# Multiplying the first 256 tokens of a softplus layer in whole fp32, and splitting its operands for later blocks only

## The chip, the cores and the metric

One core of one Trainium2 chip runs the whole program. The metric is the device time in microseconds (us), the median of several executions. Lower is better. "The profile" is the record of one execution by the hardware profiler.

## What is computed

Three layers, all on 1536 tokens (2 sequences of 768). First a gated linear recurrence per head (8 heads of 48) with a complex decay; its output is the x of the next layer. Then a feed-forward layer with softplus between its two products, and last four experts with relu, weighted per token:

```python
for t in range(S):
    S_re, S_im = ar * S_re - ai * S_im + kv, ar * S_im + ai * S_re
    y[:, :, t] = np.einsum('bhd,bhde->bhe', q[:, :, t], S_re)
...
h = x @ w_in
g = np.maximum(h, 0.0) + np.log1p(np.exp(-np.abs(h)))
x = g @ w_out
...
for e in range(4):
    out += p[:, e:e + 1] * (np.maximum(x @ w1[e], 0.0) @ w2[e])
```

Everything is fp32. d_model is 384, the softplus layer is 2048 wide, each expert 1024.

## The kernel before, in words

**Stages.** The work of the two feed-forward layers is cut into twelve stages k (k 0 to 5 for the first sequence, 6 to 11 for the second; s = k % 6). s 0 and 1 are the two halves of the softplus layer's 2048 columns, s 2 to 5 the experts. A stage has eight slices f of 128 columns and two blocks of 384 tokens; stage 0 alone has three blocks of 256 tokens, since the recurrence is still delivering its chunks of 128 tokens while it runs. Block 0 is the first 256 tokens.

**Split products.** TensorE multiplies in fp32r. To keep fp32's accuracy, each operand is a sum of a high and a low half, and a product is three matmuls (high x high, low x high, high x low). `part` (L179) makes the halves of a weight: ScalarE casts it to the high half (L181), VectorE subtracts that from the weight (L182). `done` (L718) does the same for x, out of PSUM (L721, L722), and `second` (L265) for the softplus values g (L275, L276). The recurrence itself (transposes L674, scores L683, mixes L699, states L710, prefix sums L593) multiplies in whole fp32.

**A stage's steps.** `step` (L366) runs `first` (the first product, L232, into the PSUM tile h, which holds a pair of slices f in stage 0; then |h|, exp and log on ScalarE and the maximum and sum on VectorE, L250), `second` for the step before (the split of g), and `third` for the step three before (the second product, L314, into the tile y). `low_sum` (L258) adds up one slice of g as a check.

**Weights.** The softplus weights come from memory as 64-bit numbers. `conv` (L195) joins the two words of each into an fp32 number with three VectorE operations (`join`, L69, into a scratch tile f of two buffers), splits it, and writes the joined number to a scratch tensor in memory (L200), from where stages 6 and 7 read it again. A weight of 768 columns (n even: first product, "A"; n odd: second product, "B") is converted in two halves of 384. High and low lie together in one of nine slots (NR) of a ring; three of stage 1's weights lie in a separate pool.

**Order.** The program is one list of units, sorted by a position written out by hand (`events`, `put`, `run`, L758 to L767), and each engine works through its instructions in that order. Position p is the p-th step of stage 0 for p from 0 to 24 (8 to a block); stage 1 begins at 24, stage 2 at 40. The weights of stage 0 are loaded at -5.2 + 1.6n and converted 0.4 and 0.8 later, those of stage 1 from 8.3 + 2.3n, each not before its slot is free by `ring` (L845 to L854). The recurrence's chunks are put between by position too (L863 to L868); each chunk's x comes out of `done`. All loads here are issued by SP, in the same order.

Of the kernel before, what the change touches and what calls it, by code (L numbers as in the profile page):

```python
# [9 lines left out]
F32 = mybir.dt.float32  # L10
F32R = mybir.dt.float32r
# [9 lines left out]
LAG = 3  # L21
# [15 lines left out]
NR = 9  # L37
# [38 lines left out]
def fast_path(ctx: ExitStack, tc, bad, wsc, qkv, a_re, a_im, w_in, w_out, probs, w1, w2, out):  # L76
# [83 lines left out]
    def weights(k, n, tile):  # L160
        s, which, j = k % 6, n % 2, n // 2
        nm = f"{'AB'[which]}{k}_{j}"
        z = {}

        def slot():
            t = tile([P, 2, KT, 256] if which == 0 else [P, 2, 2, DM], F32R, nm)
            W[k, n] = t
            z["d"] = t.rearrange("p s a b -> p s (a b)")

        def load():  # L170
            slot()
            if s >= 2:
                src = (w1, w2)[which][s - 2, j]
            else:
                src = wsc[s * 8 + n]
            z["raw"] = tmp.tile([P, 768], F32, tag="raw", name="raw" + nm, bufs=4)
            nc.sync.dma_start(z["raw"], src)

        def part(src, sl):  # L179
            hi, lo = (z["d"][:, i, sl] for i in range(2))  # L180
            nc.scalar.copy(hi, src)  # L181
            nc.vector.tensor_tensor(lo, src, hi.bitcast(F32), ALU.subtract)  # L182

        if k >= 2:
            return [load, lambda: part(z["raw"], slice(0, 768))]

        def load2():
            slot()
            z["raw"] = []
            for h in range(2):  # L190
                raw = tmp.tile([P, HW, 2], I32, tag="raw", name=f"raw{nm}_{h}", bufs=4)
                nc.sync.dma_start(raw.rearrange("p a w -> p (a w)"), w_raw[which][s * 4 + j, h])
                z["raw"].append(raw)

        def conv(h):  # L195
# [22 lines left out]
    def gemm1(k, blk, f):  # L218
# [10 lines left out]
        n = 0  # L229
        for kk in range(KT):  # L230
            for (p, q) in ((0, 0), (1, 0), (0, 1)):
                nc.tensor.matmul(ps, wt[:, p, kk, o:o + P], XB[b][:, q, kk, tok], start=(n == 0), stop=(n == 3 * KT - 1))  # L232
                n += 1
        return ps

    def first(k, blk, f):
# [4 lines left out]
        if k % 6 < 2:  # L241
# [7 lines left out]
            act(t, t, AF.Ln, bias=b_one)  # L249
            nc.vector.scalar_tensor_tensor(t, h, 0.0, t, ALU.max, ALU.add)  # L250
# [14 lines left out]
    def second(k, blk, f):  # L265
# [3 lines left out]
        if k == 0:  # L269
            if f % 2 == 0:  # L270
                return
# [19 lines left out]
    def third(k, blk, f):  # L291
# [15 lines left out]
        for j in range(nj):  # L307
            for n, (p, q) in enumerate(((0, 0), (0, 1), (1, 0))):
                if s < 2:
                    l_, r_ = wt[:, q, f % 2, j * P:(j + 1) * P], g[p] if k == 0 else g[:, p, :]  # L310
                else:
                    l_, r_ = g[:, p, j * P:(j + 1) * P], wt[:, q, f % 2, :]
                mate = k == 0 and j == 1
                mm = nc.tensor.matmul(ys[j], l_, r_, start=(opens and n == 0 and not mate),  # L314
                                      stop=(closes and n == 2), skip_group_check=k == 0)
# [33 lines left out]
    def closing(j):  # L349
# [4 lines left out]
        for i, sl in enumerate(parts):  # L354
            ps = psum.tile([P, 512], F32, tag="a" if i == 0 else "h", name=f"ya{j}_{i}", bufs=3 - i)[:, :sl.stop - sl.start]
            for f in range(HALF, FH):
                wt = W[k, f // 2 * 2 + 1]
                for n, (p, q) in enumerate(((0, 0), (0, 1), (1, 0))):
                    nc.tensor.matmul(ps, g_t[k, blk, f][:, p, j * P:(j + 1) * P], wt[:, q, f % 2, sl],  # L359
# [57 lines left out]
    def part(k, j, q):  # L417
# [3 lines left out]
        def prod(ps, w, x, start=False, stop=False):  # L421
            lt, li = (raws, w) if w < 5 else (sums, w - 5)
            for n, (p, r) in enumerate(((0, 0), (1, 0), (0, 1))):
                rhs = XC[b][:, r, x, :] if isinstance(x, int) else halves(b, *x, r)
                nc.tensor.matmul(ps, lt[:, p, li, :], rhs, start=(start and n == 0), stop=(stop and n == 2),  # L425
# [48 lines left out]
    def fast_weights(k, n):  # L474
# [4 lines left out]
        def load():  # L479
            z["raw"] = tmp.tile([P, 768], F32, tag="raw", name="raw" + nm, bufs=4)  # L480
            nc.sync.dma_start(z["raw"], (w1, w2)[which][s - 2, j])
            t = slot([P, 2, KT, 256] if which == 0 else [P, 2, 2, DM], F32R, nm)
            if which == 1:
                W[k, n] = t
                z["d"] = t.rearrange("p s a b -> p s (a b)")
            else:
                z["d"] = t.rearrange("p s a b -> p (s a b)")[:, :10 * P].rearrange("p (s i c) -> p s i c", s=2, i=5)
# [5 lines left out]
        def second_layer():  # L493
            split(z["d"][:, 0], z["d"][:, 1], z["raw"])

        def plain():
            r, d = z["raw"].rearrange("p (a b) -> p a b", a=KT), z["d"]
            split(d[:, 0, 0:3], d[:, 1, 0:3], r[:, :, :P])
            split(d[:, 0, 3:5], d[:, 1, 3:5], r[:, 0:3:2, P:])

        def sums():
# [9 lines left out]
            W[k, n] = (z["d"], t)  # L511
# [143 lines left out]
    def s3_units(n, c):  # L655
# [62 lines left out]
        def done():  # L718
            hi, lo = (XB[b][:, i, :, cc * P:(cc + 1) * P] for i in range(2))
            ysr = z["y"][:, :3 * P].rearrange("p (j t) -> p j t", t=P)  # L720
            nc.scalar.copy(hi, ysr)  # L721
# [46 lines left out]

    s1_load(0)
# [34 lines left out]
    def slot(shape, dt, nm):  # L804
        return wp.tile(shape, dt, tag="w", name=nm, bufs=NR)

    def spare(shape, dt, nm):
        return early.tile(shape, dt, tag=nm, name=nm)
# [4 lines left out]
    for m, k in enumerate(ORDER):  # L813
# [27 lines left out]
        for n in range(8):  # L841
            if k == 0:
                pos, gap = -5.2 + 1.6 * n, 0.4
            elif k == 1:
                pos, gap = 8.3 + 2.3 * n, 0.6  # L845
            else:
                pos, gap = base[m - 1] + 1 + 1.7 * n, 1.5
            in_early = k == 1 and n in (2, 3, 4)
            if not in_early:
                if len(ring) >= NR:  # L850
                    pos = max(pos, ring[len(ring) - NR] + 0.1)
                ring.append(base[m + 1] - FH + 2 * (n // 2) + 1 + (LAG if n % 2 else 0))
            for i, u in enumerate(weights(k, n, spare if in_early else slot)):
                events.append((pos + gap * i, len(events), u))  # L854
    for pos, need, last, k, n in sorted(fast_events):
        pos = max(pos, ring[len(ring) - NR] + 0.1)
        ring.append(last)
# [305 lines left out]
```

## Time and profile before

| | us |
|---|---|
| median of 3 executions | 736.29 (735.73 to 737.26) |
| span of the profiled execution, first to last instruction | 736.2 |
| TensorE busy | 703.0 (95%) |
| VectorE busy | 584.7 (79%) |
| ScalarE busy | 487.0 (66%) |

The profile lists no other time of its execution than the span. PE is TensorE, PEld its weight loads, DVE VectorE, ACT ScalarE, POOL GpSimd, SP the queue that issues most transfers. TensorE's records overlap one another, and their ends are modelled, so a busy share near 100% is not TensorE at its peak; the time from one record's start to the next one's is the better price. A whole-fp32 matmul (other than a transpose) has two records, an fp32r matmul one.

### The profile page before, as it was taken

To read this page: it belongs to the slowest core of one execution; us is meant where nothing else is said; L and a number is where in the kernel's file an instruction comes from. 1 tells how busy PE (TensorE), PEld (TensorE's weight loads), DVE (VectorE), ACT (ScalarE), POOL (GpSimd) and SP (SyncE) were. 2 spreads that over 40 slices of the span, in tenths; PEclk is the share of its full clock that TensorE was granted. 3 is DMA by queue.
4 is the path that set the end of the run, shared out by engine and by line. 5 is a ranking of instruction groups with operands and counts; after the bars stand their busy time and mean duration, and the time that the engine had idled before them with its cause. 6 is when DMAs were issued, how large, how long until landed. Compare 5 with 4: busy or idle time off the path is not lost.

```text
span 736.2 us, 13313 instructions
## 1 busy us (share of the span) xinstructions
PE 703.0 (95%) x5171; PEld 676.2 (92%) x5171; DVE 584.7 (79%) x1150; ACT 487.0 (66%) x898; POOL 33.3 (5%) x31
## 2 busy tenths in 40 slices
PE   1688999999999999999999999999999999999996
PEld 0477899999899999999999999999999999999996
DVE  6999999955875854648888779988788899988963
ACT  7887886878896856345686666555556667666640
POOL 1132010000111011000000000000000000000000
PEclk9699999999999999999999999999999999999998
DMA  7655666721211420121022130213454445554501
GB/s 264 195 175 170 230 190 195 228 84 44 75 55 59 122 81 2 59 86 44 23 86 65 29 102 21 87 44 98 128 159 146 137 151 172 151 172 140 172 32 69
DMA packets 36486, 83.56 MB, mean 113 GB/s; under 512 B 4544, under 2 KB 13376, under 8 KB 36416
## 3 DMA queue, kind: packets, MB, share of 16 engines
q1 hardware_dynamic: 36128, 82.35, 35.5%
q8 instruction: 42, 0.69, 0.4%
q10 hardware_dynamic: 288, 0.30, 0.1%
q14 instruction: 28, 0.23, 0.1%
HBM read 73.95 MB, written 8.65 MB: 112 GB/s over the span
## 4 chain that ended last, share of the span: by engine, by line
PE 70%; DVE 10%; DMA 9%; ACT 8%; issue 2%; POOL 1%; SPq 0%; ACTq 0%; POOLq 0%; DVEq 0%
PE y L314 21%; PE h L232 18%; PE z L314 9%; PE px L425 7%; PE pv L425 3%; PE tp L674 2%; DMA rawB<-in_w_dram 2%; DMA chkw<-in_w_in_dram 2%; PE pc L425 2%; PE sp L683 2%; PE yps L699 2%; DMA chki<-in_a_im_dram 1%; PE ya L359 1%; PE sps L710 1%; DVE fA L72 1%
## 5 line engine op out<-in xcount | busy, mean ns | idle before, releaser
L232 PE MATMUL h<-X,A 128*128 128x384 f32 (+1 forms) x936 | 176.1, 329 | 2.5 <-ACT A L181 0.8
L232 PEld LDWEIGHTS h<-X,A 128*128 128x128 f32 x936 | 153.4, 188 | 5.8 <-issue 1.6
L314 PE MATMUL y<-B,g 128*128 128x384 f32 x744 | 150.0, 335 | 0.0
L314 PEld LDWEIGHTS y<-B,g 128*128 128x128 f32 x744 | 131.1, 188 | 0.5 <-issue 0.2
L314 PE MATMUL y<-g,B 128*128 128x384 f32 (+1 forms) x504 | 91.0, 315 | 0.3 <-ACT g L285 0.3
L314 PE MATMUL z<-B,g 128*128 128x384 f32 x372 | 84.7, 334 | 0.0
L314 PEld LDWEIGHTS y<-g,B 128*128 128x128 f32 x504 | 79.3, 189 | 1.9 <-ACT g L285 0.6
L314 PEld LDWEIGHTS z<-B,g 128*128 128x128 f32 x372 | 66.3, 188 | 0.0
L247 ACT ACTIVATE e<-h 128x384 f32<-128x384 f32 (+1 forms) x60 | 30.8, 513 | 37.3 <-PE h L232 36.3
L250 DVE SCALAR_TENSOR_TENSOR e<-h,e 128x384 f32<-128x384 f32 (+1 forms) x60 | 34.9, 581 | 21.0 <-ACT e L103 20.1
L255 DVE SCALAR_TENSOR_TENSOR g<-h,g 128x384 fp32r<-128x384 f32 x32 | 17.7, 554 | 28.2 <-ACT g L254 28.2
L103 ACT ACTIVATE e<-e,b_one 128x384 f32<-128x384 f32 (+1 forms) x60 | 38.2, 637 | 1.3
L103 ACT ACTIVATE e<-e 128x384 f32<-128x384 f32 (+1 forms) x60 | 32.8, 547 | 1.3
L425 PE MATMUL px<-X,sA 128*128 128x384 f32 x144 | 33.7, 339 | 0.0
L425 PE MATMUL px<-XC,sA 128*128 128x384 f32 x144 | 33.0, 337 | 0.1
L314 PE MATMUL z<-g,B 128*128 128x384 f32 x144 | 32.9, 335 | 0.0
L674 PE MATMUL tp<-ident,QK 128*96 128x128 f32 x192 | 27.3, 290 | 5.9 <-DVE QK L665 5.0
L674 PEld LDWEIGHTS tp<-ident,QK 128*96 128x96 f32 x192 | 22.4, 133 | 10.0 <-DVE QK L665 6.2
L254 ACT ACTIVATE g<-h 128x384 fp32r<-128x384 f32 x32 | 15.6, 487 | 21.3 <-PE h L232 21.1
L286 DVE TENSOR_TENSOR g<-e,g 128x384 fp32r<-128x384 f32 x48 | 26.7, 555 | 3.8 <-ACT g L285 3.0
L490 ACT CAST B<-rawB 128x768 fp32r<-128x768 f32 x24 | 20.0, 835 | 14.1 <-DMA rawB<-in_w_dram 7.6
L490 ACT CAST A<-rawA 128x384 fp32r<-128x384 f32 (+1 forms) x48 | 20.3, 457 | 11.6 <-DMA rawA<-in_w_dram 9.2
(204 smaller groups left out, 1424.4 us busy)
## 6 DMA issues: line engine op xcount, KB each, us to landing
rawA<-in_w_dram SPq DMA_DIRECT2D x32, 384.0 KB, 3.0
rawB<-in_w_dram SPq DMA_DIRECT2D x32, 384.0 KB, 3.1
rawA<-in_w_in_dram SPq DMA_DIRECT2D x16, 384.0 KB, 3.7
rawB<-in_w_out_dram SPq DMA_DIRECT2D x16, 384.0 KB, 3.8
chkw<-in_w_in_dram SPq DMA_DIRECT2D x16, 384.0 KB, 3.5
chkw<-in_w_out_dram SPq DMA_DIRECT2D x16, 384.0 KB, 3.3
qk<-in_qkv_dram SPq DMA_DIRECT2D x12, 384.0 KB, 3.3
v<-in_qkv_dram SPq DMA_DIRECT2D x12, 256.0 KB, 3.1
```

Of the source, the lines that this page charges most:

```text
L103: i = nc.scalar.activation(out_, in_, fn, **kw)
L232: nc.tensor.matmul(ps, wt[:, p, kk, o:o + P], XB[b][:, q, kk, tok], start=(n == 0), stop=(n == 3 * KT - 1))
L247: nc.scalar.activation(t, h, AF.Abs)
L250: nc.vector.scalar_tensor_tensor(t, h, 0.0, t, ALU.max, ALU.add)
L254: nc.scalar.activation(g[:, 0, :], h, AF.Relu)
L255: nc.vector.scalar_tensor_tensor(g[:, 1, :], h, 0.0, g[:, 0, :].bitcast(F32), ALU.max, ALU.subtract)
L286: nc.vector.tensor_tensor(g[:, 1, :], t, g[:, 0, :].bitcast(F32), ALU.subtract)
L314: mm = nc.tensor.matmul(ys[j], l_, r_, start=(opens and n == 0 and not mate), stop=(closes and n == 2), skip_group_check=k == 0)
L425: nc.tensor.matmul(ps, lt[:, p, li, :], rhs, start=(start and n == 0), stop=(stop and n == 2), skip_group_check=True)
L490: nc.scalar.copy(hi, src)
L674: nc.tensor.transpose(tp[:96, hh, :], src[:, hf * 4 + hh, :], ident)
L683: nc.tensor.matmul(sp[:, hh, :], kT[:, hh, :], qT[:, hh, :], start=True, stop=True)
```

## The change

- In stage 0's block 0, x, the weights and g stay whole: `gemm1`, `third` and `low_sum` multiply them as fp32, one matmul in the place of three. `done` for the recurrence's first two chunks only copies x into a new tile `xw`; `first` writes g straight into its tile, and `second` has nothing to split.
- Stage 0's weights are joined into a whole tile (`whole`, two halves as before, each then written to memory), and split later by a new unit `apart`, 768 columns at once, at positions 6.5, 8.5, 10.5, 12.5 (first product) and 9.5, 11.5, 13.5, 15.5 (second product). Block 0's x is split once, 768 columns, at position 8.3 (`split_x`).
- High and low halves are two tiles rather than one, so the ring has 18 slots of 768 columns instead of 9 double ones. A whole weight or the whole x takes one.
- Stage 1's weights are loaded from 10 + 2.2n (converted 0.6 and 1.2 later) and the separate pool holds its n 0, 1, 2 instead of 2, 3, 4. By the ring's rule the load of stage 2's n = 4 moves from 33.1 to 38.1 and that of n = 5 from 36.1 to 37.1; the others of stage 2 and 3 keep their positions.

The diff, cut to its core (the rest adapts the indexing of high and low to two tiles):

```diff
-NR = 9
+NR = 18
...
+        def whole(h):
+            if h == 0:
+                z["f"] = wp.tile([P, 768], F32, tag="w", name="W" + nm, bufs=NR)
+                W[k, n] = shaped(z["f"])
+            sl = slice(h * HW, (h + 1) * HW)
+            join(nc, z["f"][:, sl].bitcast(I32), z["raw"][h])
+            nc.sync.dma_start(wsc[s * 8 + n, :, sl], z["f"][:, sl])
+
+        def apart():
+            home_of()
+            part(z["f"], slice(0, 768))
+
+        if k == 0:
+            return [load2, lambda: whole(0), lambda: whole(1), apart]
...
+        if (k, blk) == (0, 0):
+            for kk in range(KT):
+                nc.tensor.matmul(ps, wt[:, kk, o:o + P], xw[0][:, kk, :], start=(kk == 0), stop=(kk == KT - 1))
+            return ps
...
+            if (k, blk) == (0, 0):
+                g = flat(tmp.tile([P, 2, WM], F32, tag="g", name="g" + nm, bufs=GB))[:, :512]
+                nc.vector.scalar_tensor_tensor(g, h, 0.0, t, ALU.max, ALU.add)
+                for i in range(2):
+                    g_t[k, blk, f - 1 + i] = g[:, i * 256:(i + 1) * 256]
+                return
...
-        nc.tensor.matmul(gs[:, :TB], one_r, hi, start=True, stop=True)
+        nc.tensor.matmul(gs[:, :TB], ones if (k, blk) == (0, 0) else one_r, hi, start=True, stop=True)
...
+            whole = (k, blk) == (0, 0)
+            for n, (p, q) in enumerate(((0, 0),) if whole else ((0, 0), (0, 1), (1, 0))):
+                if whole:
+                    l_, r_ = wt[:, f % 2, j * P:(j + 1) * P], g
...
+            if n == 0:
+                nc.scalar.copy(xw[0][:, :, c * P:(c + 1) * P], ysr)
+                return
...
+    def split_x():
+        x = flat(xw[0]).rearrange("p (a b) -> p a b", a=KT)
+        hi, lo = (XB[0][:, i, :, :2 * P] for i in range(2))
+        nc.scalar.copy(hi, x)
+        nc.vector.tensor_tensor(lo, x, hi.bitcast(F32), ALU.subtract)
+
+    def free_after(n_slots):
+        return max([ring[i] for i in range(len(ring) - NR, len(ring) - NR + n_slots) if i >= 0], default=-99) + 0.1
+
+    SPLIT_X = 8.3
+    split_at = {n: FH + 2 * (n // 2) - 1.5 + (LAG if n % 2 else 0) for n in range(8)}
+    ring += [SPLIT_X] + [split_at[n] for n in range(8)]
+    for n in sorted(split_at, key=split_at.get):
+        assert free_after(2) <= split_at[n], n
+        ring += [2 * FH + 2 * (n // 2) + 1 + (LAG if n % 2 else 0)] * 2
+    put([split_x], SPLIT_X, SPLIT_X + 0.1)
...
-                pos, gap = 8.3 + 2.3 * n, 0.6
+                pos, gap = 10 + 2.2 * n, 0.6
...
-            in_early = k == 1 and n in (2, 3, 4)
+            in_early = k == 1 and n < 3
...
+                events.append((split_at[n] if (k, i) == (0, 3) else pos + gap * i, len(events), u))
```

## Rows read from the trace of the kernel before

**Rows 1.** Busy time by stretch: PE, PEld, DVE, ACT, POOL, granted clock, DMA, GB/s.
```profile
50.40:86.80 36.40, 32.87 (x415) 28.64 (x416) 35.08 (x63) 30.28 (x52) 7.63 (x5) 1.00 0.61 196
86.80:134.90 48.10, 47.84 (x526) 45.70 (x525) 46.08 (x91) 35.67 (x70) 2.44 (x1) 1.00 0.64 201
134.90:150.00 15.10, 15.10 (x98) 14.67 (x97) 13.67 (x28) 14.30 (x31) 0.00 (x0) 1.00 0.65 210
150.00:163.00 13.00, 13.00 (x76) 13.00 (x76) 6.30 (x11) 10.22 (x20) 0.00 (x0) 1.00 0.33 92
163.00:700.00 537.00, 535.63 (x3606) 524.91 (x3605) 424.56 (x843) 346.28 (x643) 13.84 (x11) 1.00 0.30 93
```

**Rows 2.** TensorE's timeline (start, duration): block 1 begins, then stage 1.
```profile
86.76 1.24 PE L232 MATMUL h<-X,A 128*128 128x256 f32 x9
...
134.88 0.51 PE L232 MATMUL h<-X,A 128*128 128x384 f32 x2
```

**Rows 3.** TensorE's back-to-back groups: chain (start, length), timeline, and groups by shape.
```profile
102.68 1.02 PE sps L710 x48
...
109.94 0.89 PE sp L683 x8
...
113.89 1.95 PE yps L699 x64
...
118.18 1.08 PE h L232 x9
...
42.82 0.81 PE L593 MATMUL pl<-t,tri 128*128 128x384 f32 x2
...
L593 PE MATMUL pl<-t,tri 128*128 128x384 f32 x4 | 1.6, 486 | 0.0
```

**Rows 4.** Who TensorE waited for, 39 to 140 us: total, times, longest.
```profile
PE tp L674 <- DVE QK L665: 1.2, 1, 1.2
PE h L232 <- ACT A L181: 0.8, 1, 0.8
PE tp L674 <- ACT kT L675: 0.8, 1, 0.8
...
PE pf L593 <- POOL im L574: 0.4, 1, 0.4
```

**Rows 5.** The chain that ended last, pieces before block 0 (start, length).
```profile
21.04 0.47 DVE A L182
...
24.24 0.47 DVE A L182
...
43.50 0.47 DVE X L722
43.97 0.47 DVE A L182
```

**Rows 6.** VectorE's timeline (start, duration), its queue back to back.
```profile
61.55 0.68 DVE L276 TENSOR_TENSOR g<-e,g 128x512 fp32r<-128x512 f32 x1
62.15 0.55 DVE L182 TENSOR_TENSOR A<-fA,A 128x384 fp32r<-128x384 f32 x1
62.62 0.35 DVE L70 TENSOR_SCALAR fA<-rawA 128x384 int32<-128x384 int32 x1
62.89 0.95 DVE L653 SCALAR_TENSOR_TENSOR qk<-dec,qk 128x768 f32<-128x768 f32 x1
...
144.16 0.96 DVE L182 TENSOR_TENSOR A<-rawA,A 128x768 fp32r<-128x768 f32 x1
145.03 0.56 DVE L286 TENSOR_TENSOR g<-e,g 128x384 fp32r<-128x384 f32 x1
```

**Rows 7.** Weight splits' subtractions, L182 alone, by stretch: length, busy (count), clock, DMA.
```profile
14.00:50.40 36.40, 3.30 (x6) 0.77 0.59 183
50.40:86.80 36.40, 4.30 (x8) 1.00 0.61 196
86.80:90.00 3.20, 1.12 (x2) 1.00 0.50 147
```

More of the change, by code (lines that the diff above doesn't have):

```diff
@@ L163, in weights, with shaped, home_of @@
         z = {}
[L165 to L168, printed above, removed]
+        def shaped(t):
+            return t.rearrange("p (a b) -> p a b", a=KT if which == 0 else 2)
+        def home_of():
+            z["d"] = tile(nm)
+            W[k, n] = [shaped(t) for t in z["d"]]
         def load():
-            slot()
+            home_of()
             if s >= 2:
@@ L179, in part @@
         def part(src, sl):
-            hi, lo = (z["d"][:, i, sl] for i in range(2))
+            hi, lo = (t[:, sl] for t in z["d"])
             nc.scalar.copy(hi, src)
@@ L229, in gemm1 @@
         n = 0
+        if (k, blk) == (0, 0):
+            for kk in range(KT):
+                nc.tensor.matmul(ps, wt[:, kk, o:o + P], xw[0][:, kk, :], start=(kk == 0), stop=(kk == KT - 1))
+            return ps
         for kk in range(KT):
             for (p, q) in ((0, 0), (1, 0), (0, 1)):
[L232 removed]
+                nc.tensor.matmul(ps, wt[p][:, kk, o:o + P], XB[b][:, q, kk, tok], start=(n == 0), stop=(n == 3 * KT - 1))
                 n += 1
@@ L424, in prod @@
                 rhs = XC[b][:, r, x, :] if isinstance(x, int) else halves(b, *x, r)
-                nc.tensor.matmul(ps, lt[:, p, li, :], rhs, start=(start and n == 0), stop=(stop and n == 2),
+                nc.tensor.matmul(ps, lt[p][:, li, :], rhs, start=(start and n == 0), stop=(stop and n == 2),
                                  skip_group_check=True)
@@ L481, in load @@
             nc.sync.dma_start(z["raw"], (w1, w2)[which][s - 2, j])
-            t = slot([P, 2, KT, 256] if which == 0 else [P, 2, 2, DM], F32R, nm)
+            t = slot(nm)
             if which == 1:
-                W[k, n] = t
-                z["d"] = t.rearrange("p s a b -> p s (a b)")
+                W[k, n] = [x.rearrange("p (a b) -> p a b", a=2) for x in t]
+                z["d"] = t
             else:
-                z["d"] = t.rearrange("p s a b -> p (s a b)")[:, :10 * P].rearrange("p (s i c) -> p s i c", s=2, i=5)
+                z["d"] = [x[:, :5 * P].rearrange("p (i c) -> p i c", i=5) for x in t]
         def split(hi, lo, src):
@@ L510, in sums @@
             split(t[:, 0], t[:, 1], m)
-            W[k, n] = (z["d"], t)
+            W[k, n] = (z["d"], [t[:, i] for i in range(2)])
         return [load, plain, sums] if which == 0 else [load, second_layer]
@@ L767, in run @@
         events.clear()
+    xw = [wp.tile([P, KT, 2 * P], F32, tag="w", name="x0", bufs=NR)]
     s1_load(0)
@@ L802, in fast_path, with slot, spare @@
     fast_events = []
[L804 to L808, printed above, removed]
+    def slot(nm):
+        return [wp.tile([P, 768], F32R, tag="w", name=f"{nm}_{i}", bufs=NR) for i in "hl"]
+    def spare(nm):
+        return [early.tile([P, 768], F32R, tag=nm + i, name=nm + i) for i in "hl"]
+    def split_x():
[12 more added lines that the diff above has]
+    put([split_x], SPLIT_X, SPLIT_X + 0.1)
     def lag_out(k):
```

37 lines of the change are left out of this document (20 added, 17 removed).

## The prediction

> **What bounds the kernel now.** I read the busy times by stretch first. The execution profiled spans 736.23 us, 0.06 below the median of the three runs (736.29), so the sum is made against 736.3. From 86.8 us on TensorE is busy for practically every microsecond up to 700 us, at a granted clock of 1.00, the 2.4 GHz level [rows 1]: whatever is done earlier or later, the end comes when TensorE has got through its list. A change to the first softplus stage can pay in two ways only: TensorE's list gets shorter, or TensorE gets into its dense stretch sooner. Before 86.8 it is not dense. Block 0 runs from 50.4 [rows 1] to 86.76, where block 1 begins, blocks 1 and 2 from there to 134.88 [rows 2]. In block 0's stretch VectorE is busy 35.1 of 36.4 us, TensorE's own figure is 32.9 [rows 1], and that one flatters it, because its records overlap. At the pace of back-to-back groups the work is less, as follows.
>
> Prices on TensorE [rows 3]. Nine split products of 256 columns in 1.08 us: 0.12 each, so a product in three passes costs 0.36. A whole-fp32 product shows as two records; 8 records of 128 columns (4 products) take 0.89, so 0.111 a record. Two records of 384 columns take 0.81 with 0.49 for the last one's own duration, so the first took 0.33 of the engine: 0.22 for 256 columns, twice that per product, 0.44. Both rows give 0.44. That is against 0.36: **a whole product is dearer than the three split ones by 0.08.**
>
> Work in block 0's stretch: 72 first-layer matmuls (8.6 us), 45 second-layer ones, f 0 to 4 (5.4), two attention chunks (transposes 32 and scores 32 x 0.111, mixes 128 x 0.030, states 96 x 0.021: 13.0), eight prefix records (2.6), one column sum (0.3): 29.9 of 36.4. So 6.5 us are lost there. The same count for blocks 1 and 2 (144 and 144 matmuls, 34.4; two chunks, one without a state, 12.0; sums 0.6) gives 47.0 of 48.1: 1.1 lost. So TensorE waits in block 0, and the waits named are for VectorE's and ScalarE's results: QK 1.2, the split of A 0.8, kT 0.8, a prefix row from POOL 0.4 [rows 4]. The chain of waits says the same: up to the time when TensorE becomes dense it runs through VectorE, and the pieces that the change removes are on it by name: two splits of A at 21 and 24 us, the split of x and another of A at 43.5 and 44.0 [rows 5].
>
> **The change, part by part.** VectorE's price is the distance from start to start in its queue [rows 6]: 0.47 for a 384-wide subtraction, 0.60 for a 512-wide, 0.87 for a 768-wide, 0.27 for a join's first operation.
>
> *Removed from VectorE*: 16 halves of weight splits (7.5 us), four splits of g (2.4), two of x (0.9): 10.9. By the table of L182, 6 of the splits lie before 50.4, 8 in block 0's stretch, 2 behind [rows 7]; with g and x that is 3.3 us before block 0, 6.0 in it, 1.5 behind.
> *Added*: eight splits 768 wide and one of x, 9 x 0.87 = 7.8 us, of which one (position 6.5) is in block 0's stretch and 7.0 are in blocks 1 and 2.
> *Moved*: the conversions of stage 1's weights go from positions 8.3, 12.9, 15.2, 17.1 ... to an even 10 + 2.2n, where one costs 2 x (0.27 + 3 x 0.47) = 3.4 us of VectorE. At position 24 seven were done, now six and a half: 1.7 us pass to the stage behind. Their loads and scratch writes stay in the same order on SP's queue relative to their joins, a little later, and lead the use by as much as before; the load of stage 2's A2 goes from 33.1 to 38.1, six steps of 3 us ahead of its use at 44. I cost them at nothing; what hides them is that lead, and if it were gone one transfer would be exposed. Block 0's joins write into weight slots rather than into the two-buffer scratch, so none waits for a scratch write any more; that too I cost at nothing.
> *ScalarE* casts 16 x 384 and 4 x 512 columns less and 9 x 768 more (fewer in all); it isn't the fuller engine in blocks 1 and 2 [rows 1]. The two casts of x become copies of the same shape.
> *TensorE*: block 0's 144 split matmuls become 48 whole products: 48 x 0.08 = 3.9 us more, with the column sum 4.0; 39 of the 48 (3.2 with the sum) lie in block 0's stretch, 9 (0.7) in the next.
>
> **Against a page.** The rows show two records per whole product, each as long as two passes. The Trainium skill, FP8 and Floating Point Precision, TensorE Precision Notes, has true fp32 as four passes through the array; the two records agree in kind. Counted by that page alone, a product of four passes against three would take a third more than 0.36, that is 0.48, and the sum would end at 735.1 instead of 733.3. I keep 0.44, since two rows of whole products give it directly.
>
> **The sum.** (1) Block 0 begins earlier by the four pieces that the chain names, 4 x 0.47 = 1.9. Bounds: nothing, and 3.3 if all seven operations count. (2) Block 0's stretch: 29.9 + 3.2 = 33.1 of work; of the 6.5 lost I leave 1.5 (kT and POOL's row keep their 1.2, and a little). 34.6 in place of 36.4: 1.8 earlier. Bounds: no loss left, 3.3 earlier; all of it left, 3.2 later. VectorE, with 6.0 - 0.9 = 5.1 us less to do, is not what holds it there. (3) Blocks 1 and 2: TensorE 48.1 + 0.7. VectorE did 46.1 us in 48.1 [rows 1] and gets 7.0 - 1.5 - 1.7 = 3.8 more: 49.9. It needs 1.1 us more than TensorE has. The third step of the pipe runs three steps behind the first and needs g split one step ahead, so VectorE may fall behind by about a step, 48.1/16 = 3.0 us, before TensorE stands: I take nothing for it. What is then owed, 1.1 + 1.7, is paid after 134.9, where VectorE has 1.4 us free up to 150 and 6.7 up to 163 [rows 1]. So -1.9 - 1.8 + 0.7 = **-3.0: 733.3 us.** The rest of the list is unchanged.
>
> **The rivals.** *Washed out*: the waits of block 0 are mostly not the removed work but the round trips between engines (ScalarE's three activations, POOL's carry row). For it: kT and POOL's row are among the waits [rows 4]. Against it: the named pieces. If 4.5 of the 6.5 stay, the stretch is 37.6, and -1.9 + 1.2 + 0.7 = 0: 736.3.
> *Slower*: VectorE becomes the bound of blocks 1 and 2. Every new split is a cast by ScalarE and then a subtraction by VectorE, which has to wait for it in its queue, so VectorE's 2.0 us of idle time there need not go away. If they stay, it needs 49.9 + 2.0 = 51.9 against TensorE's 48.8, a lag of 3.1, just over the one step allowed, and the deferred 1.7 fall on top while stage 1's weights come due. If the lag isn't allowed at all, TensorE stands for 3.1 + 1.7 = 4.8 and the sum is -3.0 + 4.8: 738.1. It decides where a wait of TensorE for a split of A or B shows after 87 us.
> *All of it*: start earlier by 1.9, no time lost in any of the three blocks (7.6), 4.0 more work: -5.5, 730.8; with the early bound of (1), 729.4.
> *Dearer products*: each of the two records takes two passes at the split matmul's pace, 4 x 0.12 = 0.48 a product; 48 x 0.12 = 5.8 in place of 3.9, so 735.2. Both rows of whole products speak against it. It is the page's count of passes above.
> *Not what it says*: were block 0's products to cost as much as before, the 4.0 are saved: 729.3; the rows of whole products speak against that.
>
> **How the numbers follow.** A measurement of this kernel can tell 0.2%, 1.5 us, from no change. Forecast (731.5 to 734.8) 0.50; washed out (734.8 to 737.8) 0.20; dearer products 0.04; slower 0.14; all of it, or cheap products, 0.12. So faster 0.62, same 0.24, slower 0.14. The range of 8 in 10 goes from 729.6 to 738.0; the forecast's own is 731.5 to 735.
>
> **What would show it.** Right: block 0's first matmul near 48.5, block 1's near 83, stage 1's near 132; whole products at 0.44; TensorE's time lost between them down from 6.5 to about 1.5; VectorE's busy share in blocks 1 and 2 nearer 100%. Wrong: gaps of the old size in front of block 0's f 4 and f 6, or TensorE waiting for L182's late splits after 83 us, or stage 1 beginning with TensorE short of weights.

## The result, and the profile after

The changed kernel takes **744.04 us** (median of 4 executions, 743.70 to 744.51) against 736.77 for the kernel before (4 executions, 735.73 to 737.42): ratio 1.0102, 95% interval 1.0087 to 1.0116. It is slower by 7.3 us, where 3.0 us faster was forecast, and 6 us above the upper end of the range. The profiled execution spans 742.8 us against 736.2; the 6.6 us between the two are looked for in these.

First the busy times by stretch: the early part, block 0, blocks 1 and 2, stage 1, the rest to 700 us. Columns as in [rows 1]. The kernel after:

```profile
14.00:39.00 25.00, 14.67 (x75) 9.51 (x75) 16.30 (x23) 19.98 (x32) 6.13 (x6) 0.66 0.36 118
48.46:89.87 41.41, 34.62 (x376) 28.39 (x377) 39.50 (x74) 27.46 (x44) 8.62 (x5) 1.00 0.82 263
89.87:140.67 50.80, 49.41 (x523) 46.75 (x522) 50.21 (x93) 40.31 (x76) 2.05 (x1) 1.00 0.60 193
140.67:196.20 55.53, 54.65 (x320) 53.78 (x319) 33.09 (x59) 47.93 (x92) 0.00 (x0) 1.00 0.27 83
196.20:700.00 503.80, 501.25 (x3415) 491.74 (x3414) 401.43 (x798) 319.11 (x591) 13.09 (x11) 1.00 0.30 94
```

The kernel before, cut at its own borders (its block 0 and blocks 1 and 2 are in [rows 1]):

```profile
14.00:39.00 25.00, 14.90 (x93) 9.97 (x97) 23.28 (x42) 20.64 (x33) 4.35 (x4) 0.66 0.63 197
134.88:190.20 55.32, 55.06 (x323) 53.88 (x322) 36.33 (x68) 48.93 (x94) 0.00 (x0) 1.00 0.34 106
190.20:700.00 509.80, 508.69 (x3455) 498.72 (x3454) 408.22 (x815) 321.88 (x599) 13.84 (x11) 1.00 0.31 95
```

The account of the 6.6: block 0 begins 1.9 earlier (48.46 against 50.37), takes 41.4 in place of 36.4 (+5.0), blocks 1 and 2 take 50.8 in place of 48.1 (+2.7), stage 1 +0.2, from stage 2's start to the end 546.6 in place of 546.0 (+0.6). In block 0 TensorE is idle 6.8 us of its stretch, where it was 3.5 [rows 1]. Who it waited for, 39 to 200 us of the kernel after (total, times, longest):

```profile
PE h L250 <- DVE WA L72: 3.3, 2, 1.9
PE tp L709 <- DVE QK L700: 2.2, 2, 1.4
PE pf L628 <- POOL im L609: 1.2, 1, 1.2
PE y L349 <- ACT g L317: 0.9, 1, 0.9
PE y L349 <- DVE g L274: 0.6, 1, 0.6
PE yps L734 <- DVE A L719: 0.6, 1, 0.6
PE h L250 <- ACT x L757: 0.5, 1, 0.5
```

The longest is new: block 0's products wait for the **joins** of its weights (WA, L70 to L72). Between 14 and 39 us VectorE is busy 16.3 of 25 us, where it was 23.3, and the transfers 0.36 in place of 0.63. The timelines show why. VectorE's first join in the kernel before, and then, in the kernel after, ScalarE's first copy of x, VectorE's first join and SP's next load of a first-layer weight:

```profile
14.87 0.35 DVE L70 TENSOR_SCALAR fA<-rawA 128x384 int32<-128x384 int32 x1
```
```profile
40.38 0.48 ACT L757 COPY x<-yps 128x384 f32<-128x384 f32 x1
...
41.96 0.61 DVE L70 TENSOR_SCALAR WA<-rawA 128x384 int32<-128x384 int32 x2
...
46.20 1.05 SPq L195 DMA_DIRECT2D rawA<-in_w_in_dram  x2
```

The first join runs at 41.96 instead of 14.87, after x's first copy (40.38), and the second first-layer weight is loaded at 46.20. The tile x0 is made first from the weight ring, ahead of all weights, and is first written when the recurrence delivers. In this build a ring hands out its slots in the order in which the program makes the tiles, so all eight joined weights, the first two with their raw data loaded, queue behind a tile that nobody could write yet.

Whole products, from start to start on TensorE's timeline (6 records are 3 products):

```profile
84.78 1.56 PE L250 MATMUL h<-x,WA 128*128 128x256 f32 x6
86.18 1.46 PE L349 MATMUL y<-g,WB 128*128 128x256 f32 x6
87.47 1.46 PE L250 MATMUL h<-x,WA 128*128 128x256 f32 x6
88.77 1.46 PE L349 MATMUL y<-g,WB 128*128 128x256 f32 x6
```

1.29 us for three: 0.43 each, as priced (0.44).

### The profile page after: what moved, and what is told of

Same layout as the page of the kernel before. It is cut to its first block, busy times and chain, and to the rows that moved or that the text cites. A ratio compares the mean times of both kernels' runs of the same rounds, so it can differ in the third digit from the quotient of the medians.

```text
span 742.8 us, 13202 instructions
## 1 busy us (share of the span) xinstructions
PE 704.2 (95%) x5124; PEld 676.2 (91%) x5124; DVE 579.5 (78%) x1137; ACT 486.0 (65%) x887; POOL 32.7 (4%) x31
## 3 DMA queue, kind: packets, MB, share of 16 engines
q1 hardware_dynamic: 36128, 82.35, 35.1%
## 4 chain that ended last, share of the span: by engine, by line
PE 60%; DVE 17%; ACT 11%; DMA 8%; issue 3%; POOL 0%; SPq 0%; ACTq 0%; DVEq 0%
PE y L349 18%; PE h L254 15%; PE z L349 8%; PE px L460 7%; PE pv L460 3%; DMA rawA<-in_w_dram 3%; PE pc L460 2%; DMA chkw<-in_w_in_dram 2%; ACT L97 2%; PE tp L709 1%; ACT t L103 1%; PE yps L734 1%; DVE QK L700 1%; ACT chkv L975 1%; PE sp L718 1%
## 5 line engine op out<-in xcount | busy, mean ns | idle before, releaser
L254 PE MATMUL h<-X,A_h 128*128 128x384 f32 (+1 forms) x528 | 146.4, 334 | 0.0
L349 PE MATMUL y<-B_h,g 128*128 128x384 f32 x496 | 146.1, 335 | 0.0
L254 PEld LDWEIGHTS h<-X,A_h 128*128 128x128 f32 x528 | 95.4, 188 | 2.4 <-issue 1.8
L349 PEld LDWEIGHTS y<-B_h,g 128*128 128x128 f32 x496 | 91.3, 188 | 0.1
L254 PE MATMUL h<-X,A_l 128*128 128x384 f32 (+1 forms) x264 | 86.4, 327 | 0.0
L349 PE MATMUL y<-B_l,g 128*128 128x384 f32 x248 | 83.0, 335 | 0.0
L349 PE MATMUL z<-B_h,g 128*128 128x384 f32 x248 | 82.9, 334 | 0.0
L349 PE MATMUL y<-g,B_h 128*128 128x384 f32 (+1 forms) x272 | 72.0, 318 | 1.0 <-ACT g L317 0.9
L349 PEld LDWEIGHTS y<-g,B_h 128*128 128x128 f32 x272 | 48.6, 189 | 1.6 <-ACT g L317 1.2
L254 PEld LDWEIGHTS h<-X,A_l 128*128 128x128 f32 x264 | 49.8, 189 | 0.1
L349 PE MATMUL z<-B_l,g 128*128 128x384 f32 x124 | 41.4, 334 | 0.0
```

Source lines behind the costliest of these rows:

```text
L254: nc.tensor.matmul(ps, wt[p][:, kk, o:o + P], XB[b][:, q, kk, tok], start=(n == 0), stop=(n == 3 * KT - 1))
```

## The experiments

Line numbers are those of each kernel. All ratios are to the kernel before on the same chip, with their 95% interval. The borders are the first matmul of block 0, of block 1 and of stage 1 on TensorE's timeline; "idle" is the length of a stretch less TensorE's busy time in it (block 0; blocks 1 and 2; stage 1; stage 2's first relu to 700 us). A border is not a clean cut: in e7 and e15 eight more of TensorE's records (533 against 525) lie behind block 1's first matmul than in the kernel before, about 1.0 us at 0.12 each.

| kernel | block 0 | block 1 | stage 1 | blocks 1+2 take | idle | span |
|---|---|---|---|---|---|---|
| before | 50.4 | 86.8 | 134.9 | 48.1 | 3.5, 0.2, 0.3, 1.1 | 736.2 |
| after | 48.5 | 89.9 | 140.7 | 50.8 | 6.8, 1.4, 0.9, 2.6 | 742.8 |
| e1 | 51.1 | 88.1 | 138.3 | 50.2 | 2.5, 1.8, 0.9, 3.5 | 742.6 |
| e5 | 50.5 | 87.4 | 138.9 | 51.5 | 2.5, 3.0, 0.3, 2.0 | 741.0 |
| e4 | 50.1 | 86.0 | 137.9 | 51.9 | 4.2, 2.8, 0.9, 5.0 | 744.4 |
| e13 | 50.4 | 85.1 | 135.2 | 50.2 | 5.6, 1.8, 1.0, 2.9 | 739.8 |
| e12 | 50.1 | 87.1 | 140.7 | 53.6 | 2.4, 3.8, 0.9, 3.7 | 744.1 |
| e14 | 52.6 | 87.2 | 137.7 | 50.5 | 2.1, 2.0, 0.3, 3.0 | 741.4 |
| e10 | 49.9 | 97.2 | 149.9 | 52.6 | 10.6, 2.7, 0.9, 3.3 | 753.9 |
| e2 | 49.3 | 91.6 | 142.3 | 50.7 | 6.4, 2.7, 0.4, 0.6 | 742.3 |
| e3 | 50.5 | 88.9 | 143.6 | 54.7 | 2.8, 4.9, 0.6, 0.8 | 744.5 |
| e6 | 50.3 | 86.4 | 134.2 | 47.8 | 3.3, 0.1, 0.3, 1.6 | 735.1 |
| e7 | 49.6 | 85.7 | 136.9 | 51.2 | 3.3, 2.4, 0.9, 2.0 | 737.8 |
| e11 | 50.6 | 86.0 | 135.8 | 49.8 | 3.5, 1.7, 1.0, 0.9 | 736.8 |
| e15 | 49.2 | 86.4 | 141.2 | 54.8 | 3.7, 4.7, 0.7, 0.6 | 741.2 |
| e16 | 49.8 | 85.9 | 135.3 | 49.3 | 3.2, 1.3, 0.9, 1.4 | 737.1 |

### The ring: e1 and e2

e1 takes x0 out of the weight ring:

```diff
-    xw = [wp.tile([P, KT, 2 * P], F32, tag="w", name="x0", bufs=NR)]
+    xw = [early.tile([P, KT, 2 * P], F32, tag="x0", name="x0")]
```

> The changed kernel, with one edit: the whole x of block 0 (x0) has a place in the separate pool of stage 1's early weights, so it no longer stands at the head of the weight ring. Theory 1 (the head of the ring): the tiles of a ring get their slots in the order in which the program makes them, and x0 is made first but first written only by the first chunk's done; so all eight weight joins of stage 0 were put behind that in VectorE's queue (first join at 42 us, VectorE busy only 16.3 of the 25 us from 14 to 39). It expects the first join back near 15 us, VectorE above 21 us busy in 14 to 39, and block 1's first matmul (89.9 us in the changed kernel) earlier by 4 us or more: a time of 733 to 738. Theory 2 (TensorE's dearer products): the 4.0 us of added matmul time and the late splits are the loss; it expects block 1 no earlier than 88 and a time of 741 or more. Theory 3 (late splits hold TensorE in blocks 1 and 2): block 1 begins earlier, but stage 1 no earlier than in the changed kernel, 742 to 744.

e2 puts the same block into the kernel before: a tile x0, made first from the ring and written (8 columns) only when the first two chunks' x is there.

```diff
+            if n == 0:
+                nc.scalar.copy(x0[:, 0, 0, c * 8:c * 8 + 8], ysr[:, 0, :8])
...
+    x0 = wp.tile([P, 2, KT, 256], F32R, tag="w", name="x0", bufs=NR)
...
-    ring = []
+    ring = [8.3]
```

> The kernel before, with one edit: a tile is made at the head of the weight ring before all others, and done for the first two chunks also writes eight columns of it (two tiny copies on ScalarE); the planner's list of slots has one entry more at its head. No product and no split is changed. Theory 1 expects the splits of stage 0's weights (L182; the first at 21 us before) to move behind the first chunk's done, near 43 us, VectorE idle in between as in the changed kernel, and a time longer than before by 3 to 9 us: 740 to 746. Theories 2 and 3 expect no more than the price of two tiny copies: 736 to 738.

Measured: e1 744.36 us, 1.0092 (1.0061 to 1.0124); e2 742.75, 1.0077 (1.0055 to 1.0099). The early stretch of e1 and its first join on VectorE's timeline:

```profile
14.00:39.00 25.00, 13.68 (x52) 8.49 (x52) 24.97 (x42) 20.73 (x33) 5.38 (x5) 0.73 0.66 207
```
```profile
15.13 0.35 DVE L70 TENSOR_SCALAR WA<-rawA 128x384 int32<-128x384 int32 x1
```

The same stretch of e2, and its first split of a weight:

```profile
14.00:39.00 25.00, 14.64 (x82) 9.69 (x86) 17.52 (x29) 19.70 (x31) 6.09 (x5) 1.00 0.52 161
```
```profile
43.44 0.54 DVE L182 TENSOR_TENSOR A<-fA,A 128x384 fp32r<-128x384 f32 x1
```

With x0 in its own place the joins are back at 15.1 us, and VectorE is busy all the 25 us; with the block alone in the kernel before, its first split goes from 21 us or sooner [rows 5] to 43.4, and the kernel is 5.7 us slower. e2 has the changed kernel's pattern, too: block 0 begins 1.1 earlier than before and takes 42.3. So the delay by the ring is shown, and that it can cost 5.7. But in the changed kernel its removal gives 1.8 us at block 1's start (88.1 against 89.9) and nothing that can be measured at the end: block 0 now begins at 51.1, since VectorE has the joins to do before it, and what is left of the gain goes in stage 1 and behind it.

### The moved loads: e7 and e5

e7 is the kernel before with the new positions of stage 1's loads; e5 is e1 with the old ones.

```diff
-                pos, gap = 8.3 + 2.3 * n, 0.6
+                pos, gap = 10 + 2.2 * n, 0.6
...
-            in_early = k == 1 and n in (2, 3, 4)
+            in_early = k == 1 and n < 3
```

> The kernel before with one edit: stage 1's weights are loaded from 10 + 2.2n and the separate pool holds its n 0 to 2, as in the changed kernel; nothing else. Theory 'the moved loads cost': the kernel with x0 in a place of its own gave back 1.6 us of its profiled span and 0.7 us at stage 2's start when its loads were put back, so the move alone costs 0.7 to 1.6 us, ratio 1.001 to 1.002, and the loss lies behind stage 1's start (softplus 16 of the list at 152 to 153 as before, stage 2's first relu at 191 to 192 in place of 190.2). Rival 'nothing, as costed': ratio 0.999 to 1.001 and stage 2's first relu within 0.5 of 190.2. A third way: by a new order of the queues alone it is 3 us slower or more, ratio over 1.004.

> The kernel with x0 out of the ring, with one part of the change undone: stage 1's weights are loaded from 8.3 + 2.3n again, and n 2, 3, 4 (not 0, 1, 2) lie in the separate pool. Theory 4 (the moved loads cost at the step from stage 1 to stage 2, where this kernel lost another 1.3 us: ScalarE casts three weights there in the stretch where before cast one or two) expects the 1.3 us back: relu of stage 2 begins 3.4 rather than 4.7 us behind before, time 742 to 743. If the loads don't matter: 744 to 745.

Measured: e7 739.99, 1.0035 (1.0021 to 1.0048): 2.6 us for a move that was costed at nothing. e5 743.31, 1.0104 (1.0072 to 1.0136), its span 1.6 below e1's, which the interval doesn't confirm. e7's waits of TensorE behind block 0, 87 to 200 us:

```profile
PE yps L699 <- DVE A L684: 1.3, 1, 1.3
PE y L314 <- ACT g L285: 0.9, 1, 0.9
PE pf L586 <- ACT hl L580: 0.9, 1, 0.9
PE gs L260 <- ACT g L275: 0.8, 1, 0.8
```

The kernel before, in the same stretch:

```profile
PE pf L586 <- ACT hl L580: 0.4, 1, 0.4
PE y L314 <- ACT g L285: 0.3, 1, 0.3
PE h L232 <- DVE e L250: 0.2, 1, 0.2
```

The waits at stage 1's end for g (L285) and hl are those that the changed kernel and e1 show (0.9 and 0.9 to 1.0), and in e5 they are down to 0.3 and 0.7. No wait for a load is named: the lead of the transfers did hide them. What moved with them are their joins, casts and splits in the queues of VectorE and ScalarE, and it is results of these two engines that TensorE waits for.

### The storage alone: e16

The kernel before with halves in two tiles and a ring of 18, nothing else of the change:

```diff
+WHOLE = (False, False)
...
-        if k == 0:
+        if k == 0 and WHOLE[which]:
             return [load2, lambda: whole(0), lambda: whole(1), apart]
```

> The kernel before with only the change's storage: high and low halves are two tiles in a ring of 18 slots; block 0's products are split ones, the weights and x are split as before, the loads are at their old positions. The amounts of work are those of the kernel before on every engine. Theory 'the storage is free': 735.5 to 738 beside 736.5 to 737.6 of the kernel before, ratio 0.998 to 1.002, and TensorE waits 1 us or less behind stage 2's start, as before. Rival 'the storage is what costs behind stage 2's start': all kernels with two tiles have 2.0 to 5.0 us of idle TensorE from there to 700 us, those with one tile 0.6 to 2.0; then some 1 to 2 us slower, ratio 1.001 to 1.003, with a wait of TensorE for he (L501 there). Rival 'any new order of the queues costs': blocks 1 and 2 take 50 to 55 us instead of 48.1, and the ratio is over 1.003.

Measured: 738.67, 1.0022 (1.0005 to 1.0038), some 1.6 us. Not by the rival named: from stage 2's start to the end it takes 546.0, as the kernel before. What it lost by then is 0.9 (191.1 against 190.2): block 1 began 0.8 earlier, blocks 1 and 2 took 1.2 more (49.3) and stage 1 0.5 more. The 1.2 can be followed in the traces. In both kernels GpSimd has one operation in blocks 1 and 2, and VectorE goes through the same list of operations beside and behind it. The kernel before, and then e16 with TensorE's longest wait there:

```profile
102.73 2.44 POOL L547 TENSOR_TENSOR t<-t,t 128x768 f32<-128x768 f32 x1 [24.21 <-ACT t L546]
102.90 0.56 DVE L71 SCALAR_TENSOR_TENSOR fA<-rawA,fA 128x384 int32<-128x384 int32 x1
```
```profile
101.83 1.94 POOL L583 TENSOR_TENSOR t<-t,t 128x768 f32<-128x768 f32 x1 [24.14 <-ACT t L582]
101.99 2.19 DVE L72 SCALAR_TENSOR_TENSOR fA<-rawA,fA 128x384 int32<-128x384 int32 x1
115.33 0.86 PE L735 MATMUL yps<-A,v 128*32 128x128 f32 x24 [1.05 <-DVE A L720]
```

The same join operation takes 0.56 us in the one and 2.19 in the other. VectorE was 0.9 ahead of the kernel before until then and is 0.7 behind from there on; it has no idle time before the recurrence's A, for which TensorE waits 1.05. It is like this in every kernel of the table but the kernel before and e6: one VectorE operation beside GpSimd's in blocks 1 and 2 (two in e10) takes 1.6 to 2.6 us, which takes 0.35 to 0.95 elsewhere. In e7 it is a join of 2.00 us, 13 us ahead of its wait of 1.3 for A. That this is what these kernels lose there was not tested by a run that moves GpSimd's operation.

### VectorE's work: e11, e12, e10

e11, the kernel before without the sixteen subtractions for the weights' low halves (stage 0 takes the high half twice); e12, e1 without the eight late ones (the same); e10, e1 with the late ones on GpSimd.

```diff
             nc.scalar.copy(hi, src)
-            nc.vector.tensor_tensor(lo, src, hi.bitcast(F32), ALU.subtract)
+            if k:
+                nc.vector.tensor_tensor(lo, src, hi.bitcast(F32), ALU.subtract)
```
```diff
-            part(z["f"], slice(0, 768))
+            nc.scalar.copy(z["d"][0], z["f"])
```
```diff
-            part(z["f"], slice(0, 768))
+            hi, lo = z["d"]
+            nc.scalar.copy(hi, z["f"])
+            nc.gpsimd.tensor_tensor(lo, z["f"], hi.bitcast(F32), ALU.subtract)
```

> The kernel before without VectorE's sixteen subtractions that make the low halves of stage 0's weights (7.5 us of VectorE, six of them before block 0 and eight in its stretch); the matmuls take the high half in the place of the low one, so TensorE's list is the same. It leaves out the weights' low parts in stage 0. Theory of the prediction, 'the pieces named on the chain are what the time goes into': block 0 begins some 1.4 earlier (three pieces of 0.47) and loses up to 2 less in its stretch, so block 1 begins at 83.4 to 84.5 instead of 86.8 and the time is 733 to 734, ratio 0.995 to 0.997. Rival 'washed out': the pieces are only where the chain happened to pass, another operation is as late; block 1 begins at 85.8 to 87, the time is 735.5 to 737, ratio 0.998 to 1.0. Third, 'order': it is slower, since the instructions fall into another order.

> The changed kernel with x0 in a place of its own, without the eight late subtractions of weights (8 x 0.87 = 7.0 us of VectorE, seven of them in blocks 1 and 2); the casts stay, and stage 0's later blocks take the high half in the place of the low one. It leaves out the weights' low parts in stage 0. Theory 'VectorE's late splits bound blocks 1 and 2' (the prediction's slower rival): from block 1's first matmul to stage 1's first maximum it takes 53.7 as before instead of 55.5, and 1.8 to 3 us come off the end: 741 to 742.5. Rival 'the loss is in the order and in the joint chain of all engines': those blocks stay at 55 or more, and the time stays within 1.2 of 744.4.

> The changed kernel with x0 in a place of its own, and the eight late subtractions of weights made by GpSimd, which has 2 to 4 us of work in blocks 1 and 2, in the place of VectorE. Theory 'VectorE's late splits bound blocks 1 and 2': blocks 1 and 2 take 53.7 to 54.5 instead of 55.5, and the time is 741 to 743, if one of GpSimd's is done within 2.5 us. Rival 'order': within 1.2 of 744.4. Third: GpSimd's subtraction takes so long, or slows VectorE beside it so much, that TensorE waits for B's or A's low halves after 87 us: over 745.6.

Measured: e11 738.16, 1.0013 (0.9996 to 1.0029); e12 746.46, 1.0126 (1.0108 to 1.0143); e10 755.65, 1.0248 (1.0229 to 1.0267). Block 0 and blocks 1 and 2, of e11 and of e12:

```profile
50.64:86.03 35.39, 31.86 (x414) 28.31 (x415) 31.58 (x55) 28.50 (x49) 5.92 (x5) 1.00 0.70 213
86.03:135.79 49.76, 48.03 (x525) 45.77 (x524) 45.81 (x88) 36.61 (x72) 3.19 (x1) 1.00 0.59 185
```
```profile
50.05:87.06 37.01, 34.63 (x377) 28.55 (x377) 36.10 (x63) 31.25 (x51) 7.19 (x5) 1.00 0.83 267
87.06:140.66 53.60, 49.84 (x524) 46.87 (x523) 46.23 (x85) 38.88 (x73) 3.55 (x1) 1.00 0.58 183
```

7.5 us of VectorE less, among them three of the four pieces that the chain of waits named (not the split of x), bring block 1 forward by 0.7 and the end by nothing: block 0 begins no earlier (50.64), its stretch is 1.0 shorter, and TensorE's idle time in it is the same 3.5. Its waits, 39 to 87 us, are now for the recurrence's A (L685), 2.8 in four places, in place of a weight's cast [rows 4]. And without the late subtractions blocks 1 and 2 don't shorten, they lengthen, though VectorE has 7.4 us free in them: "VectorE's late splits bound blocks 1 and 2" falls for e1's order. The changed kernel itself was not tried without them, and its VectorE is busy 50.2 of 50.8 us there. On GpSimd they are dear. The first of them lie in block 0's stretch; GpSimd, VectorE and TensorE's waits there:

```profile
68.89 4.22 POOL L211 TENSOR_TENSOR A_l<-WA,A_h 128x768 fp32r<-128x768 f32 x1 [5.75 <-ACT A_h L210]
...
75.29 1.79 POOL L211 TENSOR_TENSOR A_l<-WA,A_h 128x768 fp32r<-128x768 f32 x1
...
80.57 1.91 POOL L211 TENSOR_TENSOR B_l<-WB,B_h 128x768 fp32r<-128x768 f32 x1
```
```profile
73.45 7.38 DVE L71 TENSOR_SCALAR fA<-rawA 128x384 int32<-128x384 int32 x1
80.86 2.04 DVE L72 SCALAR_TENSOR_TENSOR fA<-rawA,fA 128x384 int32<-128x384 int32 x1
```
```profile
PE pl L631 <- DVE A L722: 7.9, 1, 7.9
```

Four subtractions run back to back on GpSimd from 75.29, 1.8 to 1.9 us each, against VectorE's 0.96. Beside them one VectorE operation of a join takes 7.38 us, where the same line takes 0.35 as a rule, and the next one 2.04 instead of 0.55. The recurrence's A stands right behind them in VectorE's queue, and TensorE's longest wait, 7.9, is for it. This is near the third way of the expectation: VectorE is slowed beside GpSimd; but TensorE waits for the recurrence and not for low halves.

### TensorE's work: e4, e13, e3

e4 and e13 are e1 with two and with one of block 0's three contraction slices of the first product (the sum over x is left incomplete there); e3 is the kernel before with a fourth pass in 32 of block 0's products (which adds high x high twice).

```diff
-            for kk in range(KT):
-                nc.tensor.matmul(ps, wt[:, kk, o:o + P], xw[0][:, kk, :], start=(kk == 0), stop=(kk == KT - 1))
+            for kk in range(KT - 1):
+                nc.tensor.matmul(ps, wt[:, kk, o:o + P], xw[0][:, kk, :], start=(kk == 0), stop=(kk == KT - 2))
```

> The kernel with x0 out of the ring, with TensorE's extra work taken out again: block 0's first product leaves out the last of its three contraction slices (8 whole products of 0.43 us, 3.4 us of matmul time), so block 0 computes something else. Theory 2 expects the time to fall by about 3 us, from 744.4 to 741 to 742; the rest of the loss then has another cause. Theory 1' (block 0 isn't bound by TensorE there either, the carry row and the attention chain are) expects less than 1.5 us: 743 to 744.5.

> The changed kernel with x0 in a place of its own, and in block 0 only one of the three contraction slices of the first product (16 of 24 whole products fewer, 16 x 0.43 = 6.9 us of TensorE; it leaves out two thirds of the sum over x there). TensorE then has 3 us less to do in block 0 than in the kernel before. One slice less gave 2 us at block 1's start and nothing at the end. Theory 'block 0 is bound by the round trips of the recurrence's chunks between the engines, so TensorE's work there is covered': no more than another 1 us at block 1's start (f 8 of the list, its first maximum at 93.8 to 95) and 743 to 745 at the end. Rival 'the dearer products are the cost': another 3 to 4 us, block 1's first maximum at 91 to 92, and 738 to 741 at the end.

> The kernel before, with TensorE's extra work alone: in block 0 of stage 0, 32 of the 48 products (all of the first layer, one of three column groups of the second) get a fourth pass, a repeat of high x high; 32 x 0.12 = 3.8 us of matmul time, close to the 3.9 by which 48 whole products are dearer. Block 0 computes something else by that; no split, no load, no position is changed. Theory 2 (the dearer products are paid in full, since TensorE's list sets the end): block 1 begins 3 to 4 us later and the time is 3 to 4.5 us over before, 740 to 741.5. Theory 1' (block 0 waits for VectorE, so there is room for 4 us of matmuls): block 1 begins no more than 1.5 later, time 736 to 738.5.

Measured: e4 744.94, 1.0111 (1.0088 to 1.0134); e13 741.37, 1.0049 (1.0031 to 1.0067); e3 748.01, 1.0161 (1.0135 to 1.0187). Block 0 of e13, and its waits for 39 to 87 us:

```profile
50.40:85.07 34.67, 29.04 (x345) 24.23 (x345) 31.59 (x54) 26.87 (x43) 10.67 (x5) 0.95 0.72 236
```
```profile
PE tp L709 <- DVE QK L700: 3.8, 1, 3.8
PE yps L734 <- DVE A L719: 1.9, 2, 1.7
PE pf L628 <- POOL im L609: 1.0, 1, 1.0
```

3.4 us of TensorE's work less bring block 1 forward by 2.0 (and the end by nothing), 6.9 less by 3.0 (and the end by about 3); block 0 begins 1.1 and 0.7 earlier than in e1, and its own stretch is 1.0 and 2.3 shorter. Two things take the rest. TensorE waits 2.1 and 3.8 us for the recurrence's QK, where e1 doesn't. And soon after that wait its granted clock falls to the 1.2 GHz level for about 3.4 us in both, where e1 has 1.00 all through block 0 (e13):

```profile
58.00:60.00 2.00, 2.00 (x12) 1.96 (x10) 1.69 (x2) 1.48 (x3) 1.10 (x1) 0.50 0.46 183
```

The 16 transposes and 16 scores there take 5.3 us from start to start, 3.6 by the prices of [rows 3]: some 1.7 of what was taken away went into the clock. So a part of the dearer products' 3.4 to 3.9 us does show at block 1, and these two runs don't settle how much; the waits for the recurrence are there in every one of these kernels. In the other direction, 3.8 us more in the kernel before make block 1 late by 2.2 only, but blocks 1 and 2 longer by 6.6, with new waits there, behind the longest of which the clock is at the 1.2 GHz level again (0.50 from 122 to 124 us):

```profile
PE yps L699 <- DVE A L684: 2.4, 2, 2.1
PE h L232 <- DVE e L250: 1.9, 1, 1.9
```

### The order: e6, e14, e15

e6 moves the loads of stage 0's weights by a tenth of a step; e14 (on e5) and e15 (on the kernel before) move the units of the middle and last chunks 0.6 earlier. In these two the middle chunks' first unit stands ahead of its group's trigonometry and multiplies by unfinished angles.

```diff
-                pos, gap = -5.2 + 1.6 * n, 0.4
+                pos, gap = -5.1 + 1.6 * n, 0.4
```
```diff
-    put(back(1), -0.7, 6.3)
+    put(back(1), -1.3, 5.7)
...
-    put(back(2), 8.3, 15.7)
+    put(back(2), 7.7, 15.1)
```

> The kernel before with a change that should cost nothing: stage 0's weights stand at -5.1 + 1.6n instead of -5.2 + 1.6n. It shows how much the time moves when only the order within each engine's queue is shuffled a little, since that order is worked out when the kernel is built and not written by hand. All theories expect 735.5 to 738.5; if it moves by 3 us or more, differences of that size between the other kernels prove nothing by themselves.

> The changed kernel with x0 in a place of its own and stage 1's loads as before, and the units of the recurrence's middle and last chunks put 0.6 of a step (1.8 us) earlier in the list. Theory 'what is lost in blocks 0 to 2 is the place that the chunks' steps (QK, A, kT, qT) get in the queues of VectorE and ScalarE': TensorE's waits for A, QK, qT and X between 39 and 140 shrink from some 5 to under 3 us and the time is 739 to 742. Rival 'the waits move to whatever is then late': the sum of these waits stays, and the time is within 1.2 of 743.3 or longer.

> The kernel before with the same units 0.6 of a step earlier, nothing else. Theory 'the hand-written order of the kernel before is a fitted one, and nearly any move of its units costs some microseconds': 738 to 743, ratio 1.002 to 1.009, with new waits of TensorE for A, QK, kT or g in blocks 0 to 2. Rival 'order matters only at named places': ratio 0.998 to 1.002. If the chunks' steps are simply too late in the kernel before as well, it is faster, 733 to 736.

Measured: e6 736.38, 0.9995 (0.9982 to 1.0008): a small move is free. e14 743.07, 1.0078 (1.0048 to 1.0108), with TensorE's waits for A, QK, qT and X hardly shorter (4.5 from 39 to 140 us, 5.2 in e5; for A alone 3.7 and 3.0): the place of the chunks is not what could be won back. e15 746.34 (742.93 to 748.78), 1.0129 (1.0095 to 1.0162); its profiled execution, the fastest, spans 5.0 more than that of the kernel before: blocks 1 and 2 take 6.7 longer, and TensorE waits 3.1 there for e, the softplus maximum that frees its tile h; its granted clock is 0.97 there.

## Why the prediction was wrong

**The step that failed first** is the one on moved work: "Block 0's joins write into weight slots rather than into the two-buffer scratch, so none waits for a scratch write any more; that too I cost at nothing." They wait for something else, a slot behind x0, 27 us long. It is in the diff: x0 is made from the ring before anything else, and its first writer is the recurrence. The prediction counted the ring's capacity and not the order in which it is handed out. It is not the only step that failed: without it (e1) the end is no earlier. The forecast 3.0 rested on steps 1 and 2, and they fail without it too.

**Step 1** (block 0 begins 1.9 earlier) came out to the tenth, 48.46, by luck: VectorE was free because the joins had not begun, and the ring's block alone in the kernel before brings that start 1.1 forward (e2). Where they are in their place, block 0 begins at 51.1 (e1), and with 7.5 us of VectorE's work gone at 50.6 (e11). Three of the four pieces that the chain named, gone in e11, were worth nothing there; the fourth, the split of x, was not taken away alone. The chain shows which operation came last; e11 shows that when it is taken away another, A, is as late.

**Step 2** (34.6 in block 0) was wrong by 6.8. The size of the work was right: 0.43 a product. What failed is "of the 6.5 lost I leave 1.5": 3.5 us less of VectorE's work in block 0 (e11) leave TensorE's idle time there at 3.5 and make the stretch 1.0 shorter, and the waits that are left are for the recurrence's results, A, QK and POOL's row. Nor was VectorE's busy 35.1 all work: three of its join operations beside GpSimd's take 1.25, 2.13 and 1.36 us, where one takes 0.55 elsewhere, 3.1 us too much together. That was the rival *washed out* in its mechanism (its stretch of 37.6 is near e1's 36.9), but the ring's wait came on top. The count of four passes in the Trainium skill, FP8 and Floating Point Precision, TensorE Precision Notes, would make that 0.48 a product, an estimate at the split matmul's 0.12 a pass; the trace has three in 1.29 us. Four passes of 0.107 would give that time as well, so what the trace decides is the price and not the count.

**Step 3** took 48.1 + 0.7 for blocks 1 and 2, as if TensorE's dense stretch would stay dense. It took 50.8. (Its count of the work there is a little low: 288 matmuls at 0.12 are 34.6, not 34.4.) The *slower* rival gave the right sign by a mechanism that the runs don't show: no wait for a split of A or B is named after 87 us, and e12 speaks against it in e1's order. What is shown is that this stretch of the kernel before, with 0.2 us idle, is matched only by e6: all others in the table take 49.3 to 54.8 there, whichever part was changed, and even where work was only taken away (e11, e12). The kernel before and e6 are also the only ones in which no VectorE operation takes longer beside GpSimd's there; in the changed kernel one takes 1.67 us in place of 0.55. That term stood in no sum.

**Costed at nothing or not at all**: the moved loads, 2.6 alone; the storage in two tiles, 1.6 alone.

**What can't be summed.** On the kernel before, the ring alone costs 5.7, the loads 2.6, the storage 1.6, 3.8 us of matmul 12, against 7.3 for all of the change. The prices of single parts are prices of a disturbed order, each starting from one that fitted. **Open** is the rest in e5, which has neither the ring's block nor the moved loads and is still slower, by 7.7 us by its ratio and by 4.8 in its profiled execution, its fastest. Against the forecast that execution begins block 0 2.0 late, takes 2.3 more for block 0 and 2.7 more for blocks 1 and 2, and loses 0.8 behind them. The dearer products, the storage (up to 1.6) and the VectorE operation held beside GpSimd's (2.12 us in place of 0.55) are in it; how they share the loss no run separates. Splitting only the first or only the second product's operands late would halve the change; that was not tried. No version beat the kernel before; e6 is its equal, and e11 can't be told from it.

## What to carry to other kernels

When a tile is added to a shared ring, ask who writes it first and what is made from the ring after it: a tile that waits for late data holds up all that follow, though slots are free. Before a named operation on the chain of waits is priced at its duration, ask which other result would be as late without it; in a stretch that is held by round trips between engines, an engine's work can be removed without any gain. Look for operations that take longer than their kind beside another engine's work, before a busy share is read as work. And where a hand-fitted stretch loses only a few tenths of a microsecond, a change of the queues' contents there is to be costed at a loss, here from nothing (e6) to 9 us (e15), not at the sum of its durations.

## What the runs showed of the hardware

GpSimd's subtraction of 128x768 took 1.79 to 1.91 us in the four that ran back to back in e10, about twice VectorE's 0.96 [rows 6]. The Trainium skill, GPSIMD Engine Reference, Engine selection, has two-input elementwise work at about half of VectorE's speed there; these rows agree, and one with VectorE at work beside it took 4.22. VectorE operations beside GpSimd's were held up in turn: 7.38 us in place of 0.35 in e10, 2.19 in place of 0.56 in e16. TensorE's granted clock from 14 to 39 us was 0.66 in the kernel before (a mean of the levels 1.2 and 2.4 GHz), and 1.00, the 2.4 GHz level throughout, in e6, whose TensorE was busy as long (15.17 against 14.90 us). Block 0 of e6 began 0.1 earlier (50.28 against 50.37): the clock is not what holds that start. In block 0 of e4 and e13 and in blocks 1 and 2 of e3 and e15 the clock fell to 1.2 GHz for about 3.4 us, each time at the end of a wait of 2.1 to 3.8 us or soon after it.
